# Zero products in the opening of an attention and two-layer kernel: another source, another size, and a later place for the gate sums

## The chip, the cores and the metric

The kernel runs on one core of a Trainium2 chip. The metric is the device time of one execution, in microseconds (us): lower is better. The core has five engines that run their own instruction streams and wait for each other by semaphores: TensorE (PE, matrix products; PEld is its loading of weights), VectorE (DVE), ScalarE (ACT), GpSimd (POOL) and SyncE (SP, which here only issues DMAs).

## What is computed

Four batches of eight heads of causal attention with a decay from gates `f`, then two feed-forward layers over all 2304 tokens, all in float32:

```python
scores = scale * q @ k.T                       # 576 x 576 per head, head_dim 64
cum = cumsum(log(clip(f, 0.0001, 1.0)))        # the gate sums
scores = where(causal, -1e9, scores + cum[:, None] - cum[None, :])
attn = softmax(scores) @ v
x = attn as (2304, 512)
x = leaky_relu(x @ w_in) @ w_out               # 512 -> 2048 -> 512, slope 0.01
out = silu(x @ w2_in) @ w2_out
```

## The kernel before, in words

Python code records the instructions while a small event simulation (class `Plan`) runs: each step says on which engine it runs, a rank and a planned cost, and the simulation decides the order in which steps stand in each engine's stream. The chip then executes these fixed streams. A changed planned cost or a new wait in the recording code therefore changes the order of instructions far beyond the edited line.

When the PE stream would be idle in the simulation, `Plan.issue` records a "filler" instead: a product of zeros into a PSUM tile `fps` that nobody reads. The filler has a planned cost in `p.filler["pe"]`, and once it is over the simulation looks again for real work. On the chip a filler is an ordinary instruction: what stands behind it waits until it is done.

The opening goes like this. `gates` loads the gates (`fs`), takes their logarithm on ACT, and sums them over positions by products with a triangle of constants `tri` (tile `cps`, line 435), in two halves of the sequence: the first 256 positions and the other 320. Both results go through `plain_rows` into `cum_p`, a DRAM row from which later heads load their decay. The first `DIRECT` = 2 heads do not wait for that: `score` adds the decay by further products with `fs` and `tri` (lines 674 and 676, tile `sps`). Other heads compute scores by line 683. DVE takes the maximum out of `sps` (line 663), ACT the exponential (line 706), PE transposes the result (line 765, tile `tps`), and PE multiplies it by the values (line 835, tile `av`). The first eight heads, rows 0 to 255 of batch 0, are done like this before the first product of the first layer (line 965, tile `hps`), which waits for all eight (`wait(("weighed", H - 1))`). The scores of heads 8 and 9, the first two of the next half, are also largely done before it. Meanwhile DVE and ACT convert the weights of the first layer.

Most real products of the opening are float32: each is recorded as two instruction pairs, a load of weights and a product. Products of the first layer use fp32r, one pair each.

Fillers run in two kinds. From the start, `z`, a 128x256 tile that DVE sets to zero, is multiplied by its own first 128 columns (line 398). Once the mask tile `zmask` is complete and the first block of head 0 is scored, 128 zero columns of `zmask` are multiplied with themselves (line 401). They end with the first `hps` product group.

Of the kernel before, what the change touches and what calls it, by code (L numbers as in the profile page):

```python
# [9 lines left out]
F32 = mybir.dt.float32  # L10
F32R = mybir.dt.float32r
# [22 lines left out]
DIRECT = 2  # L34
# [40 lines left out]
class Plan:  # L75
# [39 lines left out]
    def op(self, eng, cost, fn, rank=1, lat=None):  # L115
        def step(resume):
            self.count += 1
            heapq.heappush(self.ready.setdefault(eng, []), (rank, self.count, cost, fn, lat, resume))
            self.at(self.now, lambda: self.issue(eng))

        return step
# [36 lines left out]
    def dma(self, nbytes, fn, rank=1):  # L158
        return self.op("sp", 0.64, fn, rank, nbytes / 360e3)

    def wait(self, *names):
        def step(resume):
            missing = [n for n in names if n not in self.seen]
            if not missing:
                resume()
                return
            left = [len(missing)]

            def one():
                left[0] -= 1  # L170
                if not left[0]:
                    resume()

            for n in missing:
                self.waiting.setdefault(n, []).append(one)

        return step
# [8 lines left out]
    def signal(self, name):  # L186
        self.seen[name] = True
        for fn in self.waiting.pop(name, []):
            fn()

    def take(self, pool, bufs):


        def step(resume):
            i = self.taken[pool] = self.taken.get(pool, -1) + 1
            if i < bufs or (pool, i - bufs) in self.given:
                resume(i)
            else:
                self.queue[pool, i - bufs] = lambda: resume(i)

        return step

    def give(self, pool, i):
        self.given[pool, i] = True
        fn = self.queue.pop((pool, i), None)
        if fn:
            fn()
# [16 lines left out]
def seq(*steps):  # L224
    for step in steps:
        yield step
# [14 lines left out]
def pe_cost(n, passes=1):  # L241
    return passes * n / 2360
# [3 lines left out]
def fused_kernel(ctx, tc, qt, kt, va, vb, ft, w1, wi2, wo2, out):  # L246
    nc = tc.nc
# [12 lines left out]
    p = Plan()  # L260
    op, dma, wait, take, give, signal, par = p.op, p.dma, p.wait, p.take, p.give, p.signal, p.par
# [22 lines left out]
    def f32(ap):  # L284
        return ap.bitcast(F32)
# [8 lines left out]
    def act(n, fn, rank=1, base=0.09):  # L294
        return op("act", act_cost(n, base), fn, rank)

    def dve(n, fn, rank=1, fast=False):
        return op("dve", dve_cost(n, fast), fn, rank)
# [82 lines left out]
    def gates(cp):  # L381
        nfull = S // 128
        rem = S - nfull * 128
        parts = ((128, slice(0, nfull)), (rem, slice(nfull, nfull + 1)))
        fs = cp.tile([128, nfull + 1, H * B], F32, name="fs")
        tri = cp.tile([128, HALF[1][1]], F32, name="tri")
        cp3 = cp.tile([H * B, 2, S], F32, name="cp3")
        cr = cp.tile([H * B, 4, S], F32R, name="cr")
        warm = cp.tile([1, 1], F32, name="warm")
        z = cp.tile([128, 256], F32R, name="z")  # L390
        opened.update(tri=tri, fs=fs, parts=parts, ones=(cp3[:, 0, :], f32(cr[:, 0:2, :])))

        def fillers():
            yield op("dve", 0.28, lambda: nc.vector.memset(f32(z), 0.0), 0)
            i = yield take(("acc", 1), 1)
            fps = ps_acc.tile([128, 256], F32, tag="acc1", name="fps")
            none = zmask[:, 0:128]
            p.filler["pe"] = 0.2, lambda: nc.tensor.matmul(fps, z[:, 0:128], z, start=True, stop=True)
            p.issue("pe")
            yield wait("zmask", ("scored", 0, 0))  # L400
            p.filler["pe"] = 0.21, lambda: nc.tensor.matmul(fps[:, 0:128], none, none, start=True, stop=True)  # L401
            yield wait(("hid", 0, 0))
            del p.filler["pe"]
            give(("acc", 1), i)

        def logs(k):
            n, sl = parts[k]
            if k:
                yield dma(8e3, lambda: nc.sync.dma_start(out=fs[0:n, nfull, :], in_=ft[nfull * 128:S, :]), -1)
            else:  # L410
                yield dma(100e3, lambda: nc.sync.dma_start(
                    out=fs[:, sl, :], in_=ft[0:nfull * 128, :].rearrange("(c p) h -> p c h", p=128)), -3)
            signal(("fs", k))
            yield wait(("clamped", k))
            yield act(128, lambda: nc.scalar.activation(fs[0:n, sl, :], fs[0:n, sl, :], ACTF.Ln), 0)
            signal(("logs", k))

        p.start(fillers())
        p.start(build_consts())
        p.start(logs(0))  # L420
        p.start(logs(1))
        p.start(seq(wait(("logs", 0), ("logs", 1)),
                    op("act", 1.4, lambda: nc.scalar.activation(warm, fs[0:1, 0, 0:1], ACTF.Exp), 0)))
        pss = []
        banks = []
        for i, (t0, tn) in enumerate(HALF):
            yield wait("tri", ("logs", i))
            banks.append((yield take(("av", "sp")[i], (1, 3)[i])))
            ps = ps_at.tile([H * B, tn], F32, tag=("av", "sp")[i], name="cps", bufs=(1, 3)[i])
            todo = [c for c in range(nfull + 1) if t0 <= 128 * c < t0 + tn]  # L430

            def sums(c):
                n = 128 if c < nfull else rem
                lo = 128 * c - t0
                nc.tensor.matmul(  # L435
                    ps[:, lo:tn], fs[0:n, c, :], tri[0:n, 0:tn - lo], start=(c == todo[0]), stop=(c == todo[-1]),
                )

            for piece in ([todo] if i == 0 else [[c] for c in todo]):
                yield op("pe", sum(pe_cost(tn - 128 * c + t0, 4) for c in piece),  # L440
                         lambda: [sums(c) for c in piece], 1 if i else -1)
            pss.append(ps)
            if i == 0:
                p.start(first_rows(ps, first_row["tile"]))
        signal("cum")

        def plain_rows():
            yield wait("rows_set")
            for i, ((t0, tn), ps) in enumerate(zip(HALF, pss)):
                w = slice(t0, t0 + tn)  # L450
                if i == 0:
                    yield act(tn, lambda: nc.scalar.copy(cp3[:, 1, w], ps), 0)
                    yield wait("cf")
                else:
                    yield dve(tn, lambda: nc.vector.tensor_scalar(
                        cp3[:, 1, w], ps, cp3[:, 1, t0 - 1:t0], None, op0=ALU.add), 0)
                give(("av", "sp")[i], banks[i])
            yield dma(147e3, lambda: nc.sync.dma_start(out=cum_p, in_=cp3), 0)
            signal("cum_p")

        def split_rows():
            c, hi, lo = cp3[:, 1], cr[:, 2], cr[:, 3]
            yield act(S, lambda: nc.scalar.copy(hi, c))
            yield dve(S, lambda: nc.vector.tensor_tensor(lo, c, f32(hi), op=ALU.subtract))
            yield dma(295e3, lambda: nc.sync.dma_start(out=cum_d, in_=f32(cr)))
            signal("cum_d")

        yield from plain_rows()
        yield from split_rows()
        yield wait(("scored", DIRECT - 1, 1))  # L470
        signal("gates")

    def first_rows(ps, cf):

        yield wait("ones")
        yield act(256, lambda: nc.scalar.copy(cf[:, 1], ps[0:H]), 0)
        signal("cf")
        yield par(*[seq(
            dma(8e3, partial(nc.sync.dma_start, out=first[i][64:65], in_=cf[2 * i:2 * i + 2]), i - H),
            signals(("row", i)),  # L480
        ) for i in range(DIRECT // 2, H // 2)])
        give("stg", first_row["i"])
        signal("rows")
# [1222 lines left out]
    cp = cum_es.enter_context(tc.tile_pool(name="cump", bufs=1))  # L1706
# [4 lines left out]
    def opening():  # L1711
        first_row["i"] = yield take("stg", STG_BUFS)
        first_row["tile"] = stg([H, 2, HALF[0][1]], F32, "cfr")
        for i in range(5):
            yield take(("w", i), 1)
        p.start(gates(cp), after_gates)
        yield from load_first()
        yield wait(*[("weighed", n) for n in range(H)])
        for i in range(5):
            give(("w", i), 0)  # L1720
# [61 lines left out]
```

## Time and profile before

| | us |
|---|---|
| median of three timed runs | 993.75 |
| the three runs | 993.75, 994.51, 987.34 |
| the profiled execution | 993.82 |
| its span, first to last instruction | 992.1 |
| PE busy | 983.7 |
| DVE busy | 772.6 |
| ACT busy | 648.0 |
| first product of the first layer starts | 44.48 |

Times in the trace count from the start of the span. The busy time of PE is modelled, since products are pipelined. In the chain of waits the piece of a group begins where the piece before it ends, so that its length is what the group added to the chain. [...]

### The profile page before, as it was taken

Reading aid. Unit: us, or ns where it says so; the run is one execution under the profiler, and the core shown is the slowest. Engines: PE = TensorE matmul, PEld = TensorE weight load, DVE = VectorE, ACT = ScalarE, POOL = GpSimd, SP = SyncE. Lnnn points to the kernel's source line nnn. Section 1 sums busy time; section 2 is a strip of 40 time slices with the busy share of each in tenths; the row PEclk is TensorE's granted clock in tenths of the full one; section 3 lists DMA queues with packets and bytes.
Section 4 is the critical chain, followed back from the end, with each engine's and each line's share of the span. In section 5 each row is a group of like instructions: output and inputs, shape, how many; then the busy total and the mean of one; then the engine's idle time right before and its main releaser. Section 6 shows DMA issues by size and latency. Waiting matters only on the chain.

```text
span 992.1 us, 20120 instructions
## 1 busy us (share of the span) xinstructions
PE 983.7 (99%) x7367; PEld 944.9 (95%) x7367; DVE 772.6 (78%) x1837; ACT 648.0 (65%) x1423; POOL 105.5 (11%) x134
## 2 busy tenths in 40 slices
PE   9999999999999999999999999999999999999998
PEld 6877779999999999999999999999999989999998
DVE  3999867878888788887876898557667779899884
ACT  4876767777788767977765567657557765445441
POOL 2000002111222222442211110000000000000000
PEclk9999999999999999999999999999999999999999
DMA  7744523231242221342221675396887984545442
GB/s 228 242 148 123 173 65 108 72 102 41 61 132 78 64 78 46 90 126 64 85 70 57 229 266 202 124 322 214 291 288 271 354 278 122 149 137 161 128 129 64
DMA packets 111831, 148.41 MB, mean 150 GB/s; under 512 B 8170, under 2 KB 89078, under 8 KB 111700
## 3 DMA queue, kind: packets, MB, share of 16 engines
q1 hardware_dynamic: 111300, 146.73, 46.7%
q8 instruction: 58, 0.95, 0.4%
q10 hardware_dynamic: 432, 0.39, 0.1%
q14 instruction: 41, 0.34, 0.1%
HBM read 98.93 MB, written 43.43 MB: 143 GB/s over the span
## 4 chain that ended last, share of the span: by engine, by line
PE 96%; DMA 1%; ACT 1%; DVE 1%; issue 0%; DVEq 0%
PE hps L965 21%; PE acc L1047 19%; PE m L1431 17%; PE m L1277 16%; PE sps L683 7%; PE tps L765 5%; PE av L876 4%; PE acc L1041 3%; PE av L835 2%; PE fps L401 1%; DMA ws<-w_d 1%; DMA g<-g_d 1%; PE sps L676 0%; PE cps L435 0%; PE sps L674 0%
## 5 line engine op out<-in xcount | busy, mean ns | idle before, releaser
L965 PE MATMUL hps<-ring,w 128*128 128x256 f32 x1728 | 261.8, 288 | 0.0
L965 PEld LDWEIGHTS hps<-ring,w 128*128 128x128 f32 x1728 | 229.3, 191 | 4.2 <-issue 2.2
L1047 PE MATMUL acc<-g,dec 128*128 128x256 f32 x1344 | 199.3, 285 | 0.0
L1047 PEld LDWEIGHTS acc<-g,dec 128*128 128x128 f32 x1344 | 177.9, 191 | 0.4
L706 ACT ACTIVATE sc<-sc,st 128x576 f32<-128x576 f32 (+4 forms) x160 | 93.2, 583 | 52.1 <-DVE st L663 50.9
L1277 PE MATMUL m<-xa,w 128*128 128x384 f32 x576 | 113.7, 339 | 0.8 <-DVE ev L1072 0.8
L1431 PE MATMUL m<-w,xa 128*128 128x256 f32 x924 | 112.5, 280 | 0.5 <-DVE xa L314 0.5
L1431 PEld LDWEIGHTS m<-w,xa 128*128 128x128 f32 x924 | 110.4, 188 | 0.7 <-DVE xa L314 0.7
L1277 PEld LDWEIGHTS m<-xa,w 128*128 128x128 f32 x576 | 101.8, 188 | 1.0 <-DVE ev L1072 1.0
L306 ACT CAST dec<-wo 128x512 fp32r<-128x512 f32 x112 | 69.5, 621 | 44.3 <-PE acc L1047 43.5
L663 DVE CUSTOM_DVE_ANT_0 sc<-sps,zmask 128x288 f32<-128x288 f32 (+4 forms) x160 | 72.0, 451 | 30.7 <-PE sps L683 16.4
L1277 PE MATMUL m<-xb,w 128*128 128x384 f32 x432 | 86.6, 337 | 0.8 <-ACT z L1332 0.8
L314 DVE TENSOR_TENSOR dec<-wo,dec 128x512 fp32r<-128x512 f32 x92 | 64.9, 705 | 20.9 <-ACT dec L306 20.4
L306 ACT CAST xa<-g 128x512 fp32r<-128x512 f32 x88 | 49.2, 567 | 46.8 <-PE m L1431 18.5
L1277 PEld LDWEIGHTS m<-xb,w 128*128 128x128 f32 x432 | 76.0, 188 | 1.6 <-ACT z L1332 1.4
L1431 PE MATMUL m<-w,xb 128*128 128x256 f32 x588 | 74.3, 283 | 0.6 <-ACT xb L306 0.4
L1431 PEld LDWEIGHTS m<-w,xb 128*128 128x128 f32 x588 | 72.0, 191 | 1.0 <-ACT xb L306 0.6
L783 DVE TENSOR_TENSOR pl<-tps,pt 107x320 fp32r<-107x320 f32 (+2 forms) x114 | 54.2, 509 | 18.0 <-ACT pt L782 17.1
L1114 DVE TENSOR_TENSOR g<-g 128x256 f32<-128x256 f32 x144 | 59.4, 420 | 10.8 <-DMA g<-g_d 10.1
L765 PE MATMUL tps<-ident,sc 66*107 66x66 f32 (+3 forms) x480 | 66.4, 268 | 0.0
L683 PE MATMUL sps<-m,s 66*128 66x288 f32 (+9 forms) x264 | 59.9, 308 | 0.0
L782 ACT CAST pt<-tps 107x320 fp32r<-107x320 f32 (+2 forms) x114 | 45.9, 446 | 18.6 <-PE tps L765 18.3
(150 smaller groups left out, 1659.2 us busy)
## 6 DMA issues: line engine op xcount, KB each, us to landing
g_d<-z SPq DMA_DIRECT2D x24, 768.0 KB
g<-g_d SPq DMA_DIRECT2D x36, 512.0 KB
w_d<-f SPq DMA_DIRECT2D x16, 896.0 KB
ws<-w_d SPq DMA_DIRECT2D x56, 256.0 KB
wst<-in_wi_dram SPq DMA_DIRECT2D x16, 512.0 KB
wst<-in_wo_dram SPq DMA_DIRECT2D x16, 512.0 KB
qk<-in_kt_dram SPq DMA_DIRECT2D x24, 288.0 KB
wss<-in_w_dram SPq DMA_DIRECT2D x10, 512.0 KB
```

Of the source, the lines that this page charges most:

```text
L306: ("act", act_cost(n, base), lambda: nc.scalar.copy(dst, src), 0.0),
L314: ("dve", dve_cost(n), lambda: nc.vector.tensor_tensor(dst, a, b, op=ALU.subtract), 0.0),
L663: yield dve(w, lambda: nc.vector.tensor_tensor_reduce(out=sc[0:qn, k0:k0 + w], in0=ps[0:qn], in1=zmask[0:qn, z0:z0 + w], scale=-0.125, sca ...
L683: nc.tensor.matmul(ps[0:qn], ht[x][:, qs], ht[y][:, k0:k0 + w], start=r == 0, stop=r == len(ops) - 1)
L706: yield act(kn, lambda: nc.scalar.activation(sc[0:qn, 0:kn], sc[0:qn, 0:kn], ACTF.Exp, scale=-1.0, bias=st[0:qn, 2 * i + a:2 * i + a + 1], ...
L765: nc.tensor.transpose(ps[0:k1 - k0, o:o + qn], ht["p"][i][0:qn, k0:k1], ident[0:qn, 0:qn])
L783: yield op("dve", dve_cost(width), lambda: nc.vector.tensor_tensor(pts[1][0:kw], ps[0:kw], f32(pt[0:kw]), op=ALU.subtract), 0, PE_LAT)
L965: nc.tensor.matmul(hp_t[:, part], w[:, wi, c * 128:(c + 1) * 128], x[xi][:, c, :], start=(part == 0 and c == 0 and r == 0), stop=(c == KC ...
L1047: nc.tensor.matmul(o, w[:, wi, c * 128:(c + 1) * 128], g[:, gi, part * T:(part + 1) * T], start=(start and r == 0 and c % 2 == 0), stop=(s ...
L1114: ("dve", dve_cost(n), lambda: nc.vector.tensor_tensor(dst, a, b, op=op_), 0.0),
L1277: nc.tensor.matmul(dst, w[:, wi, c * 128:(c + 1) * 128], x[:, xi, c], start=start and c == 0 and r == 0, stop=stop and c == 1 and r == 2, ...
L1431: nc.tensor.matmul(banks[b][:, e], t[:, gi, a * 128:(a + 1) * 128], w[:, wi], start=begin and a == 0 and r == 0, stop=jp == NP // 2 - 1 an ...
```

## The change

Four edits. The tile `z` and its setting to zero are gone: the first fillers read a constant of value 0.0 that the program's own start-up writes, as float32, 128 columns by 128, with a planned cost of 0.42 in place of 0.2. The later fillers multiply 64 columns in place of 128, against the same 128 columns of weights, with a planned cost of 0.11 in place of 0.21. The gate sums of the second half are recorded only after the scores of head 1 (`("scored", DIRECT - 1, 1)`). Lines behind these edits are numbered one higher than before, those between them one lower.

```diff
-        z = cp.tile([128, 256], F32R, name="z")
 ...
         def fillers():
-            yield op("dve", 0.28, lambda: nc.vector.memset(f32(z), 0.0), 0)
             i = yield take(("acc", 1), 1)
             fps = ps_acc.tile([128, 256], F32, tag="acc1", name="fps")
             none = zmask[:, 0:128]
-            p.filler["pe"] = 0.2, lambda: nc.tensor.matmul(fps, z[:, 0:128], z, start=True, stop=True)
+            zero = nc.const_aps.tensor(0.0, [128, 128], F32)
+            p.filler["pe"] = 0.42, lambda: nc.tensor.matmul(fps[:, 0:128], zero, zero, start=True, stop=True)
             p.issue("pe")
             yield wait("zmask", ("scored", 0, 0))
-            p.filler["pe"] = 0.21, lambda: nc.tensor.matmul(fps[:, 0:128], none, none, start=True, stop=True)
+            p.filler["pe"] = 0.11, lambda: nc.tensor.matmul(fps[:, 0:64], none, none[:, 0:64], start=True, stop=True)
 ...
             todo = [c for c in range(nfull + 1) if t0 <= 128 * c < t0 + tn]
+            if i:
+                yield wait(("scored", DIRECT - 1, 1))
```

The first place is the start of PE's stream: first fillers, gate sums (`cps`) and the scores of head 0 (`sps`; a row "x15" is fifteen equal instructions in a row, and a float32 product is one row here). Before:

```order
L398 MATMUL fps<-z 128x256 x15
L435 MATMUL cps<-tri,fs 32x256
L435 MATMUL cps<-tri,fs 32x128
L674 MATMUL sps<-qk_116 128x128
L676 MATMUL sps<-tri,fs 128x128
L435 MATMUL cps<-tri,fs 32x320
L674 MATMUL sps<-qk_116 128x256
L676 MATMUL sps<-tri,fs 128x256
L676 MATMUL sps<-tri,fs 128x128
```

After:

```order
L397 MATMUL fps<-const-float32-0.0 128x128 x8
L436 MATMUL cps<-tri,fs 32x256
L436 MATMUL cps<-tri,fs 32x128
L675 MATMUL sps<-qk_115 128x128
L677 MATMUL sps<-tri,fs 128x128
L397 MATMUL fps<-const-float32-0.0 128x128
L675 MATMUL sps<-qk_115 128x256
L677 MATMUL sps<-tri,fs 128x256
L677 MATMUL sps<-tri,fs 128x128
```

Fifteen fillers of 256 columns have become eight of 128, and a ninth stands where the 320 columns of the second gate sum stood.

The second place is PE's stream behind the last score of head 1, up to the second group of transposes (`tps`). Before:

```order
L676 MATMUL sps<-tri,fs 128x128
L401 MATMUL fps<-zmask 128x128 x3
L765 MATMUL tps<-ident,sc 128x128 x3
L401 MATMUL fps<-zmask 128x128
L683 MATMUL sps<-qk_117 128x128
L401 MATMUL fps<-zmask 128x128
L683 MATMUL sps<-qk_117 128x256
L401 MATMUL fps<-zmask 128x128 x3
L765 MATMUL tps<-ident,sc 128x128 x3
```

After:

```order
L677 MATMUL sps<-tri,fs 128x128
L400 MATMUL fps<-zmask 128x64
L436 MATMUL cps<-tri,fs 32x320
L766 MATMUL tps<-ident,sc 128x128 x3
L436 MATMUL cps<-tri,fs 32x192
L684 MATMUL sps<-qk_116 128x128
L436 MATMUL cps<-tri,fs 32x64
L684 MATMUL sps<-qk_116 128x256
L400 MATMUL fps<-zmask 128x64 x3
L766 MATMUL tps<-ident,sc 128x128 x3
```

The three pieces of the second gate sum stand here now, among the first transposes and the scores of head 2, where fillers stood.

The third place is PE's stream behind the values of heads 4 and 5 (`av`), some 10 us before the first layer begins. Before:

```order
L835 MATMUL av<-pf,v_120 64x256 x2
L401 MATMUL fps<-zmask 128x128
L835 MATMUL av<-pf,v_120 64x128 x2
L401 MATMUL fps<-zmask 128x128 x3
L765 MATMUL tps<-ident,sc 128x128 x3
```

After:

```order
L836 MATMUL av<-pf,v_119 64x256 x2
L400 MATMUL fps<-zmask 128x64
L836 MATMUL av<-pf,v_119 64x128 x2
L400 MATMUL fps<-zmask 128x64 x14
L766 MATMUL tps<-ident,sc 128x128 x3
```

Three fillers have become fourteen. Up to the first `hps` row the real PE instructions are the same ones before and after; the fillers of `zmask` number 46 before and 75 after.

## Rows read from the trace of the kernel before

**Rows 1.** The page's first part: busy time of each engine, share of the span, instructions.

```profile
PE 983.7 (99%) x7367; PEld 944.9 (95%) x7367; DVE 772.6 (78%) x1837; ACT 648.0 (65%) x1423; POOL 105.5 (11%) x134
```

**Rows 2.** Waits of PE, whole span: who for whom, total us, times, longest.

```profile
PE fps L398 <- DVE z L394: 1.3, 1, 1.3
PE m L1277 <- ACT z L1332: 0.8, 2, 0.6
...
PE m L1431 <- DVE xb L314: 0.2, 1, 0.2
```

**Rows 3.** Chain of waits, 0 to 24 us: start, length, engine, tile, line, instructions.

```profile
1.26 3.57 PE fps L398 x15
4.83 1.42 PE cps L435 x4
...
7.70 1.21 PE cps L435 x2
...
11.63 0.78 PE cps L435 x2
...
13.86 0.35 PE cps L435 x2
...
16.93 1.28 PE fps L401 x6
18.21 0.64 PE tps L765 x3
18.85 0.43 PE fps L401 x2
...
20.98 0.74 PE fps L401 x6
21.73 0.33 PE tps L765 x3
```

**Rows 4.** Chain of waits, 24 to 47 us.

```profile
26.60 0.67 PE fps L401 x6
...
42.74 1.98 PE fps L401 x16
44.72 0.71 PE hps L965 x6
```

**Rows 5.** Chain of waits, 21.73 to 44.72 us: share of that stretch by line.

```profile
by line: PE fps L401 42.8%; PE sps L683 30.6%; PE av L835 16.6%; PE tps L765 10.0%
```

**Rows 6.** Two stretches: busy us (instructions) of each engine, clock, DMA share, GB/s.

```profile
4.83:16.93 12.10, 12.10 (x31) 6.65 (x32) 1.99 (x10) 4.21 (x12) 3.12 (x8) 1.00 0.86 225
21.73:44.72 22.99, 22.99 (x163) 17.46 (x162) 21.29 (x78) 19.68 (x57) 0.00 (x0) 1.00 0.71 227
```

**Rows 7.** Timeline at 162 us, fp32r products by line 876: start, us, engine, instruction.

```profile
162.25 0.28 PE L876 MATMUL av<-pl,vh 128*128 128x256 f32 x1
...
162.37 0.22 PE L876 MATMUL av<-pt,vh 128*128 128x128 f32 x1
162.37 0.19 PEld L876 LDWEIGHTS av<-pl,vh 128*128 128x128 f32 x1
162.43 0.27 PE L876 MATMUL av<-pl,vh 128*128 128x128 f32 x1
162.48 0.42 PEld L1047 LDWEIGHTS acc<-g,dec 128*128 128x128 f32 x3
162.54 0.45 PE L1047 MATMUL acc<-g,dec 128*128 128x256 f32 x2
```

**Rows 8.** Timeline of the first 1.3 us, instructions of POOL, ACT's queue and DVE.

```profile
0.30 0.10 POOL L1770 MEMSET const-float32-0.0<- 128x1 f32 x1 [0.30 <-issue]
...
0.93 0.27 DVE L394 MEMSET z<- 128x256 f32 x1 [0.93 <-PEq L1770]
```

**Rows 9.** Timeline: issue of `cum_p`, and the first scores that read it.

```profile
16.06 0.39 SPq L458 DMA_DIRECT2D cum_p<-cp  x1
...
36.87 0.70 PE L683 MATMUL sps<-k,s 65*66 65x320 f32 x2
```

## The prediction

> **What bounds the kernel now.** The page's busy times come first: PE is busy 99% of the span, DVE 78%, ACT 65% [rows 1]. PE's waits say how much of its time is lost: 1.3 us at the start, until DVE has set `z` to zero, and then five kinds of waits between 0.8 and 0.2 us each, 2.7 us in all, in the second layer [rows 2]. So PE's stream is the path from 1.26 us on, and whatever is taken out of it or put into it moves the end by as much, unless it opens or fills a wait. The chain of waits of the opening says which parts of that stream are not needed: 3.57 us of `z` fillers, then from 16.93 us on mask fillers between the real products, and 1.98 us of them just before the first layer begins [rows 3, 4]. Between 21.73 and 44.72 us mask fillers hold 42.8% of the chain, 9.84 of 22.99 us, in 38 products [rows 5]. In the same stretch DVE is busy 21.29 us [rows 6]: shorter fillers could win only some 1.7 us there before DVE becomes the bound. Longer fillers have no such limit.
>
> [...]
>
> **The change part by part.** All against the profiled execution, 993.82 us, which is 0.07 above the median of the three runs.
>
> *The constant in place of `z`.* The constant is written at 0.30 us, and engines leave the start-up at about 0.93, where DVE begins [rows 8]. PE starts there instead of at 1.26: -0.33 us. The memset was on DVE, idle then: nothing. Eight float32 fillers of 128 columns at 0.43 [rows 3] are 3.44 us in place of 3.57: -0.13. A ninth one stands in PE's stream before the second score of head 0: +0.43 at the low clock, +0.22 at the high one.
>
> *The gate sums.* The three pieces, 1.21 + 0.78 + 0.35 = 2.34 us [rows 3], move behind the scores of head 1: PE does the same work, so the sum is zero. Behind them wait `cum_p` and, through it, the rows for heads 8 and 9. `cum_p` was issued at 16.06 and first read by a score at 36.87 us [rows 9]; about 5 us of delay fit into the 20.81 us between, and the loads of weights behind `cum_p` on SP's queue keep their order and a similar margin. If that cover were gone, PE would wait at most those 5 us once.
>
> *Mask fillers of 64 columns.* Forty-six become 75, because the planner charges 0.11 us for each and so puts about two where one stood. The question is their price. No row before has 128 columns of weights against 64 moving columns in float32. The upper bound is that of today's filler, 0.22 us (0.67 for three) [rows 4], the lower its half, 0.11. The nearest row decides for the upper one: two fp32r products of 128 columns follow each other at 162.37 and 162.43, the second is recorded 0.05 us longer than the first (0.27 against 0.22), and weight loads follow each other after 0.11 us (162.37, 162.48) [rows 7]. A load of 128 weight columns takes 0.11 us there, and only a product as long as that hides it. A float32 filler has two loads: 0.22 us whatever streams past them. I take 0.22, and 0.43 at the low clock.
>
> [...]
>
> *Where the time goes, if the clock rises at 21 us as before.* Up to the second group of transposes: PE starts at 0.93; 3.44 for the eight; the chain from 4.83 to 21.73 is 16.90 us, of which fillers 1.28 + 0.43 + 0.43 + 0.74 = 2.88, so 14.02 real; the ninth constant filler and six of the mask add 7 x 0.43 = 3.01. Together 0.93 + 3.44 + 14.02 + 3.01 = 21.40, against 21.73: -0.33. From there to the first `hps` product 75 - 6 = 69 fillers stand where 38 stood: 31 x 0.22 = +6.8 us. Sum +6.5: 1000.3 us.
>
> *If it rises early.* The base is the run of 987.34 us. Start and first fillers -0.33 and -0.13, the ninth +0.22, and 29 more mask fillers at 0.22 are +6.4: 993.5 us. That run won 6.4 us, though halving everything from 4.83 to 21 us would win 8.1, so some 1.7 us of PE's time were waits for DVE, ACT and loads; fillers that fall into these cost nothing. That gives 991.8 to 993.5, and I take 992.6.
>
> *Downstream.* The planner's new order also moves conversions between ACT, DVE and POOL in the middle of the kernel. PE has its work ready there in all but 2.7 us [rows 2]; I put it at zero, within 2 us either way.
>
> [...]
>
> **Forecast:** early rise, fillers at the price of their weight loads, 992.6 us, chance 0.50.
>
> **Rival 1, the clock rises at about 21 us.** 1000.3 us, chance 0.24. [...]
>
> **Rival 2, the clock stays low until the first layer: slower.** [...] Then the 22.99 - 9.84 = 13.15 us of real work take 26.3, and 69 fillers 29.7: the first `hps` product starts at 77.4 us and not at 44.72, +32.7. [...] It decides if the rise has not come by the time the mask fillers start. Chance 0.13.
>
> **Rival 3, the half-size filler does cost half.** Late rise: 69 x 0.11 = 7.6 against 9.84 would give -2.2, of which DVE leaves 1.7; six early ones at 0.21 save 1.3; -0.33: 990.5 us. Early rise: 987.34 - 0.33 - 0.13 + 0.22, less 1.9 for 75 x 0.11 against 46 x 0.22, gives 985.2. For it speaks only that the planner's price assumes it; against it the loads at 162 us. Chance 0.13.
>
> **How the numbers follow.** The prediction is the forecast's, 993 us rounded. About 1% is what a measurement of this kernel can tell from no change: 983.8 to 1003.7 us. The forecast, rival 3 and most of rival 1 lie within. Slower is rival 2 with 0.13, and 0.04 of rival 1 where the downstream order adds to it: 0.17. Faster needs rival 3 with an early rise and a gain downstream: 0.05. Same is the rest, 0.78. The range runs from 985, rival 3's lower end, to 1004, rival 1 with a loss downstream; rival 2 alone is outside.
>
> **What would show it.** First `hps` product, in the chain of waits: 42 to 44 us for the forecast, 51 for rival 1, 77 for rival 2, 41 or less for rival 3. A run of fourteen 64-column fillers, 28 instructions: 3.1 us by weight loads, 1.5 by columns, 6 at the low clock. The time of a 128-column transpose group behind the first scores, 0.64 or 0.33 us, shows the clock. PE's first instruction should start near 0.93 us. And PE should still show no wait before the second layer: a wait on DVE or on a DMA before the scores of heads 2 or 8 would mean that fillers are no longer the bound and their price matters less than I say. The forecast is wrong if the first layer starts where I say and the end still differs by more than 2 us: then the downstream order matters.

## Result: slower by 1.2%, and the profile after

The kernel after takes 1000.25 us (median of six runs, 999.45 to 1002.93), before 991.17 (six runs, 986.98 to 994.51): the ratio is 1.0119, 95% interval 1.0091 to 1.0147. Forecast were 993 us and no change. Before's runs lie in two groups, 987 to 989 and about 994 us, after's in one. In the later comparisons before's median is 987.6, and 72 of its 86 runs lie in the lower group; against that after loses 12.7 us.

The profiled execution took 1002.93 us, its span is 1001.2. PE is busy for longer than before [rows 1], with 61 more instruction pairs:

```profile
PE 988.9 (99%) x7428; PEld 950.4 (95%) x7428; DVE 778.5 (78%) x1839; ACT 645.5 (64%) x1418; POOL 106.8 (11%) x136
```

The chain of waits of the opening, to be held against [rows 3] (start, length, engine, tile, line, instructions):

```profile
0.85 3.75 PE fps L397 x16
4.60 1.42 PE cps L436 x4
...
7.08 0.22 PE fps L397 x2
...
11.59 0.66 PE cps L436 x2
12.25 0.48 PE tps L766 x3
...
15.06 0.33 PE tps L766 x3
```

PE starts with the constant at 0.85. The ninth constant filler takes 0.22 us at 7.08, where the eight first took 0.47 each (3.75 / 8). The second gate sum begins with 0.66 us in place of 1.21, the first transposes take 0.48 in place of 0.64, and the second ones 0.33 already at 15.06. In the profile before such transposes take 0.64 us at 18.21 and 0.33 at 21.73, and a mask filler 0.43 at 18.85 and 0.22 at 26.60 us (0.67 for three) [rows 3, 4]; the longer times are called the low clock here, the shorter ones the high clock. So TensorE left the low clock for the high one before 7.08 us, and not at about 21 us as in the profile before. The trace's own record of the granted clock, which lists 1.00 and 0.50 of full speed, begins at 1.00 at 6.4 us after and at 21.0 before, where the times get shorter; ahead of that it lists nothing.

Further on in the same chain, against [rows 4]:

```profile
26.23 2.15 PE fps L400 x18
...
32.74 3.27 PE fps L400 x28
```

Fourteen 64-column fillers, 28 instructions, take 3.27 us, 0.234 each. The timeline shows the first product of the first layer at 44.13 us, 0.35 us earlier than before (start, length, engine, instruction):

```profile
44.13 0.72 PE L966 MATMUL hps<-ring,w 128*128 128x256 f32 x4
```

What the early clock won in the opening the fillers took back. The other 9 us of this execution arose later. PE's waits (who for whom, total us, times, longest), in whose list before has nothing above 0.8 us but its start [rows 2]:

```profile
PE acc L1042 <- DVE wo L1481: 1.9, 1, 1.9
PE acc L1048 <- DVE wr L314: 1.7, 1, 1.7
PE m L1432 <- ACT xb L306: 1.0, 1, 1.0
...
PE m L1432 <- DVE xb L314: 0.7, 2, 0.4
```

Their places in the timeline of PE; the brackets hold the idle time ahead of an instruction and what ended it:

```profile
53.52 0.74 PE L1048 MATMUL acc<-g,wr 128*128 128x256 f32 x2
56.00 0.74 PE L1048 MATMUL acc<-g,wr 128*128 128x256 f32 x4 [1.73 <-DVE wr L314]
...
125.93 1.62 PE L1042 MATMUL acc<-gw,wo 128*128 128x256 f32 x3 [1.85 <-DVE wo L1481]
```

Both are products with the second matrix of the first feed-forward layer, `w_out` ("second-layer weights" in the expectations below), that wait for converted weights: `wr` are the two weight tiles that stay resident, `wo` is the eleventh of the fourteen others that DVE finishes in the first pass:

```profile
125.10 0.68 DVE L1481 SCALAR_TENSOR_TENSOR wo<-wso,ct 128x512 int32<-128x512 int32 x1
```

Here is what the windows show behind the first of them, and over a longer stretch at each (busy us of PE, PEld, DVE, ACT and POOL, then the granted clock):

```profile
56.00:57.50 1.50, 1.50 (x13) 1.50 (x14) 1.49 (x3) 1.50 (x4) 0.00 (x0) 1.00 0.00 0
57.70:61.00 3.30, 3.30 (x15) 2.10 (x14) 3.30 (x8) 2.00 (x4) 0.00 (x0) 0.50 0.00 0
61.20:65.00 3.80, 3.80 (x25) 2.91 (x24) 1.52 (x4) 0.43 (x1) 0.00 (x0) 1.00 0.86 247
...
50.00:70.00 20.00, 18.27 (x100) 12.54 (x99) 17.45 (x45) 11.23 (x25) 0.00 (x0) 0.91 0.44 148
110.00:135.00 25.00, 23.15 (x133) 17.80 (x133) 17.83 (x50) 14.71 (x34) 0.00 (x0) 0.93 0.46 151
```

After the wait, PE had worked for 1.6 us when its granted clock fell to 0.50 of full speed, at 57.6 us in the clock's record, and it came back 3.4 us later. At 0.91 of full speed over 20 us and 0.93 over 25 us, up to 1.8 us are lost at each place, by an estimate from these shares. So the two waits and the two falls make at most 3.6 + 3.5 = 7.1 of the 9.5 us that this execution is longer than before's behind the first layer's start (1002.93 - 44.13 = 958.8 against 993.82 - 44.48 = 949.3). This execution is the longest of after's six, and its mean granted clock, 0.996, the lowest; the others have 0.998 or 0.999.

### The profile page after: what moved, and what is told of

It reads as the page before. It is cut to its first block, busy times and chain, and to the rows that moved or that the text cites. A ratio compares the mean times of both kernels' runs of the same rounds, so it can differ in the third digit from the quotient of the medians.

```text
span 1001.2 us, 20230 instructions
## 1 busy us (share of the span) xinstructions
PE 988.9 (99%) x7428; PEld 950.4 (95%) x7428; DVE 778.5 (78%) x1839; ACT 645.5 (64%) x1418; POOL 106.8 (11%) x136
## 4 chain that ended last, share of the span: by engine, by line
PE 92%; DVE 3%; DMA 2%; ACT 1%; issue 1%; SPq 0%; DVEq 0%; ACTq 0%
PE hps L966 19%; PE acc L1048 18%; PE m L1278 17%; PE m L1432 16%; PE sps L684 6%; PE tps L766 5%; PE av L877 4%; PE acc L1042 2%; PE av L836 2%; PE fps L400 1%; DMA g<-g_d 1%; DMA wss<-in_w_dram 1%; PE fps L397 0%; DVE sc L664 0%; DVE g L1115 0%
## 5 line engine op out<-in xcount | busy, mean ns | idle before, releaser
L306 ACT CAST xa<-g 128x512 fp32r<-128x512 f32 x88 | 49.6, 568 | 46.0 <-PE m L1432 24.2
```

Source lines behind the costliest of these rows:

```text
L306: ("act", act_cost(n, base), lambda: nc.scalar.copy(dst, src), 0.0),
```

## The experiments

Two quantities tell the parts apart in every run: the start of the first `hps` product, and the **rest**, which is the profiled execution's time less that start. The recorded order gives two more. The fillers are those of the mask tile up to the first `hps` product. A maximum is one block of scores reduced by DVE (`sc<-sps,zmask`): counting how many stand ahead of the two `wr` and ahead of the last `wo` in DVE's stream tells how late these conversions are placed. Up to the first `hps` product PE does the same real products in every kernel, but for six transposes more (0.63 to 0.66 us) in e4 and e8.

| kernel | fillers x us each | maxima ahead of wr; last wo | first hps | PE's wait on wr, wo | rest | median |
|---|---|---|---|---|---|---|
| before | 46 x 0.22 | 22, 23; 50 | 44.48 (late clock) | 0, 0 | 949.3 | 987.6 |
| after | 75 x 0.234 | 26, 26; 54 | 44.13 | 1.7, 1.9 | 958.8 | 1000.25 |
| e1 narrow weights | 75 x 0.12 | as after | 41.34 | 1.7, 1.9 | 956.4 | 998.72 |
| e2 same order, 128 columns | 75 x 0.237 | as after | 44.29 | as after | 956.9 | 1001.60 |
| e3 no size | 47 x 0.22 | 22, 22; 50 | 38.23 | 0, 0 | 951.8 | 989.97 |
| e4 size alone | 93 x 0.22 to 0.24 | 24, 26; 56 | 47.58 | 0, 0 | 954.6 | 1001.81 |
| e5 true price | 38 x 0.22 to 0.24 | 22, 24; 54 | 35.64 | 0, 1.8 | 955.5 | 991.53 |
| e8 constant alone | 53 x 0.24 | 22, 24; 50 | 39.88 | 0, 0 | 950.1 | 989.93 |
| e9 planned at 0.13 | 80 x 0.22 to 0.24 | 22, 23; 50 | 45.00 | 0, 0.3 | 949.3 | 994.40 |
| e10 rows first | 83 x 0.22 to 0.24 | 22, 23; 50 | 45.80 | 0, 0.5 | 956.5 | 1002.23 |
| e11 rows late | 45 x 0.22 | 26 and more; 50 | 39.22 | 1.5, 0 | 956.8 | 996.11 |
| e12 before, narrow | 46 x 0.12 | as before | 38.53 | 0, 0 | 950.2 | 988.85 |
| e13 planned at 0.13, narrow | 80 x 0.12 | as e9 | 42.52 | 0, 0.3 | 949.2 | 992.03 |
| e14 no size, narrow | 47 x 0.12 | as e3 | 38.06 | 0, 0 | 952.0 | 990.18 |
| e15 conversions first | 75 x 0.22 to 0.24 | 22, 24; 50 | 43.09 | 0, 0 | 955.7 | 999.45 |
| e16 residents first | 75 x 0.22 to 0.24 | 22, 24; 52 | 43.84 | 0, 0 | 956.9 | 1000.71 |
| e17 before, conversions first | 48 x 0.22 | 21, 24; 50 | 37.32 | 0, 0 | 956.1 | 993.48 |

In all but before's profile the clock rose early, as in after: at 4.1 to 6.8 us by the clock's record. The medians are device times in us; before's is that of the runs shared with the experiments (987.58 to 988.03). The price of a filler is read from its runs in the chain at the high clock; a piece also holds what the first filler of a run waited for, so runs of five and more give 0.21 to 0.26 us with 128 weight columns and 0.12 to 0.14 with 32. The `wo` that PE waits for in after, the eleventh, stands behind 50 maxima in after, e1, e2 and e5, which wait 1.8 to 1.9 us for it, and in e4, which does not; in the other kernels it stands behind 43 to 46.

### First round: which edit, and is it the filler's price?

**e1, narrow weights.** After's order to the instruction, with a cheaper filler:

```diff
-matmul(fps[:, 0:64], none, none[:, 0:64], ...)
+matmul(fps[0:32, 0:64], none[:, 0:32], none[:, 0:64], ...)
```

> The changed kernel with the same order of every engine's instructions; only what a mask filler loads is smaller: 32 weight columns in place of 128 (64 moving columns as before, planned cost 0.11 us as before), so that it writes 32 rows of the unread tile. Theory 'price': the 64-column filler costs 0.23 us on the chip because of its two loads of 128 weight columns, twice what the order was planned with, and the real products, and DVE's and ACT's conversions behind them, run late against the plan. Then a run of 28 filler instructions, 3.3 us in the changed kernel, takes 1.5 to 2 us, the first layer starts 2 to 5 us earlier than at 44.1, the waits of PE near 55 and 125 us go, and the time is 985 to 992 us. Theory 'order': the new order of instructions itself, with the gate sums moved, lets the conversions come too late; then the filler gets cheaper, but the waits near 55 and 125 us stay and the time is 996 to 1000.

Measured: 998.72 us, ratio to before 1.0102 [1.0073, 1.0132]. The chain shows fourteen fillers in 1.68 us, half of after's price:

```profile
31.61 1.68 PE fps L400 x28
```

The first `hps` product came only 2.8 us earlier, and both waits stayed:

```profile
PE acc L1042 <- DVE wo L1481: 1.9, 1, 1.9
PE acc L1048 <- DVE wr L314: 1.7, 1, 1.7
```

So the price is a small part of the loss: 1.5 of 12.7 us.

**e2, after's order with 128 columns.**

```diff
-p.filler["pe"] = 0.11, ... matmul(fps[:, 0:64], none, none[:, 0:64], ...)
+p.filler["pe"] = 0.11, ... matmul(fps[:, 0:128], none, none, ...)
```

> The changed kernel with the same order; only the mask filler streams 128 columns again (128 weight columns, planned cost still 0.11 us). 'Price' by weight loads: the filler costs the same 0.22 to 0.23 us with 64 as with 128 columns, so the time is that of the changed kernel within 2 us (998 to 1003), first layer at 44 us. If instead columns set the price, 75 fillers of 0.11 us more put the first layer at about 50 us or later and the time at 1005 or more.

Measured: 1001.60 us, ratio 1.0133 [1.0104, 1.0162]. The same run of fourteen fillers:

```profile
32.80 3.32 PE fps L400 x28
```

With 64 columns it took 3.27 us. Half of the columns saved 0.05 us in fourteen fillers. (The first `hps` product came 0.16 us later although the clock rose 1.3 us earlier than in after, at 5.1 us; by an estimate from that, half of 1.3 us, the columns were worth some 0.8 us in all 75.)

**e3, the first and the second edit without the third** (128 columns, planned at 0.21).

```diff
-p.filler["pe"] = 0.11, ... matmul(fps[:, 0:64], none, none[:, 0:64], ...)
+p.filler["pe"] = 0.21, ... matmul(fps[:, 0:128], none, none, ...)
```

> The changed kernel without its third edit: mask fillers of 128 columns at a planned 0.21 us, constant and moved gate sums kept; 47 mask fillers up to the first layer. 'Price': plan and chip agree, the clock rises early as in the changed kernel, and the time is that of the quick runs of the kernel before or a little less, 983 to 989 us. 'Order' (the moved gate sums are what costs): 995 to 1001 us.

Measured: 989.97 us, ratio 1.0015 [0.9991, 1.0039]. No wait on `wr` or `wo`.

**e4, the third edit alone**, made in before.

```diff
-p.filler["pe"] = 0.21, ... matmul(fps[:, 0:128], none, none, ...)
+p.filler["pe"] = 0.11, ... matmul(fps[:, 0:64], none, none[:, 0:64], ...)
```

> The kernel before with the third edit alone: mask fillers of 64 columns at a planned 0.11 us, z fillers and gate sums as before; 93 mask fillers up to the first layer. 'Price': 93 at 0.23 in place of 46 at 0.24 us put the first layer some 10 us later where the clock rises at 21 us, 5 us where it rises early, and the waits behind it come: 997 to 1008 us. 'Order' (gate sums moved): the gate sums are not moved here, so no loss, 987 to 994 us.

Measured: 1001.81 us, ratio 1.0133 [1.0104, 1.0162]. The third edit alone loses more than the whole change, and behind the first two it adds 10.3 of the 12.7 us (after against e3). Half as many columns are no loss (with all of them e2 takes 1.35 us longer than after); what is left of this edit is the planned cost of 0.11 and the order that follows from it.

### Second round: the count, or the place of the conversions?

**e5, planned at the measured price.**

```diff
-p.filler["pe"] = 0.11, ... matmul(fps[:, 0:64], none, none[:, 0:64], ...)
+p.filler["pe"] = 0.23, ... matmul(fps[:, 0:64], none, none[:, 0:64], ...)
```

> Changed against the kernel after: the planned cost of the 64-column filler is 0.23 in place of 0.11, which is what it was measured to take (0.234 us). The instruction stays the same; the planner then records 38 of them before the first layer in place of 75, and places the conversions of the two resident second-layer weights (wr) behind 22 and 24 score maxima of DVE in place of 26 and 26. Theory 'planned cost' (the planner's order and count are what costs): the first hps product at 36 to 39 us, no wait of PE on wr, median 985 to 991 us. Theory 'instruction' (64 columns against 128 columns of weights are bad for PE by themselves, whatever their number): waits and falls of the granted clock as after, median 996 to 1002.

Measured: 991.53 us, ratio 1.0032 [1.0018, 1.0047]. Of after's loss 8.7 us are gone with the instruction unchanged. That is half a microsecond above the range of "planned cost". The first `hps` product is the earliest of all runs; the rest is 6.2 us above before's, with one wait on `wo`, which I had not expected:

```profile
PE acc L1042 <- DVE wo L1481: 1.8, 1, 1.8
```

**e9, planned at 0.13**, nothing else.

> Changed against the kernel after: planned cost 0.13 in place of 0.11, nothing else. By accident of the order the planner now records 80 fillers before the first layer, five more than after, but wr stands behind 22 and 23 score maxima. Theory 'late conversions' (about half of the loss is the place of the wr and wo conversions on DVE and ACT, the other half is fillers): fillers cost as after or up to 1.2 us more, the first hps product comes at 44 to 46 us, but PE does not wait on wr, and the time from the first hps product to the end is 949 to 952 us as in the kernel before and without the 64 columns, not 956 as after: median 993 to 998. Theory 'fillers alone' (what comes after the first layer's start is a consequence of the fillers, or of running them at 64 columns): 1000 to 1004, with 956 to 958 us behind the first hps product.

Measured: 994.40 us, ratio 1.0073 [1.0050, 1.0096]. Five fillers more than after, the first `hps` product 0.9 us later, and yet 5.9 us less. The rest is before's to the tenth. PE's list of waits has its start at the top, and `wr` not at all:

```profile
PE fps L397 <- PEq L1771: 0.8, 1, 0.8
PE m L1278 <- DVE ev L1073: 0.8, 1, 0.8
PE m L1432 <- DVE xa L314: 0.5, 1, 0.5
PE acc L1042 <- DVE wo L1481: 0.3, 1, 0.3
```

**e10, the second half's rows first:** the steps that the `wr` conversions wait for in the planner go ahead of others.

```diff
-yield act(S, lambda: nc.scalar.copy(hi, c))
+yield act(S, lambda: nc.scalar.copy(hi, c), 0)
 ...  # likewise rank 0 for the subtraction on DVE and the DMA of cum_d
```

> Changed against the kernel after: the three steps that write cum_d (split_rows: a copy on ACT, a subtraction on DVE, a DMA), for whose end the wr conversions wait in the planner, get rank 0 in place of 1 and so go ahead of first-layer conversions. 64 columns at 0.11 stay; 83 fillers before the first layer in place of 75; wr behind 22 and 23 score maxima. Theory 'late conversions': no wait of PE on wr, 949 to 953 us from the first hps product to the end, median 994 to 999 although there are eight more fillers. Theory 'fillers alone': eight more fillers cost 1.9 us, median 1001 to 1005, and 956 us or more behind the first hps product.

Measured: 1002.23 us, ratio 1.0142 [1.0123, 1.0161]. The `wr` moved and its wait vanished, but the rest stayed at 956.5: against "late conversions". Other waits appeared, on DVE's scaled scores and on a hidden tile:

```profile
PE tps L766 <- DVE sc L715: 1.6, 4, 0.5
...
PE hps L966 <- DVE g L314: 0.7, 1, 0.7
```

**e11, rows late**, in e3: the suspected cause added to a kernel without it.

```diff
+yield wait(("scored", 6, 1))
 c, hi, lo = cp3[:, 1], cr[:, 2], cr[:, 3]
```

> The suspected cause added alone: 128 columns at the planned 0.21 as before, the constant and the later gate sums as after, and the steps that write cum_d wait in the planner for the scores of head 6. 45 fillers before the first layer (47 without that wait), wr behind 26 score maxima and more, as after. Theory 'late conversions': the first hps product at 37 to 39 us, but PE then waits 1 to 2 us on wr and again on wo, 955 to 959 us from the first hps product to the end, median 993 to 997. Theory 'fillers alone': nothing changes against the kernel with the first two edits, 988 to 991, no such wait.

Measured: 996.11 us, ratio 1.0077 [1.0060, 1.0094], 6.1 us above e3. The wait on `wr` came (line numbers are one higher here), the one on `wo` did not, and the rest rose by 5.0 us:

```profile
PE acc L1049 <- DVE wr L314: 1.5, 1, 1.5
```

So a late `wr` goes with a loss; e10 says that an early one is no cure by itself.

### Third round: what is a filler's price worth?

The edit of e1, in three other orders: before (**e12**), e9 (**e13**), e3 (**e14**).

> The kernel before with one edit: its 46 mask fillers load 32 columns of zeros and stream 64 in place of 128 and 128; the planned cost stays 0.21, so that every instruction keeps its place. In the trace of the narrow-weights run such a filler took 0.124 us (nine in 1.12), against 0.22 for the one before. Theory 'DVE takes over': of 46 x 0.1 = 4.6 us only part comes back, since DVE was busy 21.29 of 22.99 us in that stretch; first hps product 1 to 2.5 us earlier than in an execution of before with an early rise of the clock, median 985 to 987. Theory 'fillers bind': the first hps product 4 to 4.6 us earlier, 983 to 984. Theory 'clock': narrow loads keep PE less busy, the clock rises late or falls, and the time is 990 or more.

> Both halves of the loss taken away at once: the order that the planned cost 0.13 gives (80 fillers, no wait on wr or wo; 994.4 us with the 64-column filler) and the filler with 32 weight columns (0.124 us in place of 0.234). Theory 'price and order are two separate parts': the first hps product at 41 to 43 us in place of 45.0, no wait on wr and at most 0.5 us on wo, median 990 to 992. Theory 'narrow loads do nothing once the waits are gone' (DVE binds): 993 to 995.

> The first two edits of the change, the planned cost 0.21, and the filler with 32 weight columns: the order of the kernel without the 64 columns (47 fillers, 989.97 us), at a lower price of each filler. Theory 'DVE takes over': first hps product 36 to 37.5 us in place of 38.2, median 988 to 989.5. Theory 'fillers bind': 47 x 0.1 = 4.7 us come back, first hps product 33.5 us, median 985 to 986. Theory 'clock': 991 or more, with a late rise or a fall.

Measured: 988.85 us [0.9994, 1.0018], 992.03 [1.0026, 1.0054], 990.18 [1.0006, 1.0033]. In e13 the 80 fillers give back 2.5 us at the first `hps` product, as expected there. In e12 and e14 they give nothing, where each theory had expected something ("clock" fails too: it rose at 5.7 us in e12, and both times lie below that theory's). Chain shares by line, 5 us to the first `hps` product, of e3 and then of e14, say why:

```profile
by line: PE fps L400 34.5%; PE sps L684 24.9%; PE av L836 11.5%; PE tps L766 8.4%; PE sps L677 7.6%; PE cps L436 7.6%; PE sps L675 6.3%; PE fps L397 0.7%
```

```profile
by line: PE sps L684 32.4%; PE fps L400 24.7%; PE av L836 11.5%; PE tps L766 10.2%; PE cps L436 7.8%; PE sps L677 7.7%; PE sps L675 6.3%; PE fps L397 0.7%
```

Of 33.2 and 33.1 us, the fillers fell from 11.5 to 8.2, while the scores of line 684 rose from 8.3 to 10.7 and the transposes from 2.8 to 3.4: 3.3 us less there, 3.0 more here. It isn't DVE that takes over, as I had expected, but the real product next to the filler. Pieces of the chain at the same place, of e3 and then of e14, show it:

```profile
14.61 0.33 PE tps L766 x3
14.94 0.22 PE fps L400 x2
15.16 0.22 PE sps L684 x2
```

```profile
14.58 0.48 PE tps L766 x3
15.06 0.23 PE fps L400 x2
15.29 0.42 PE sps L684 x2
```

A single filler with 32 weight columns is no cheaper than one with 128, 0.23 against 0.22 us, and the transposes ahead of it, which stand behind fillers as well, and the score behind it take 0.15 and 0.20 us longer.

**e8, the constant alone.**

```diff
-p.filler["pe"] = 0.2, lambda: nc.tensor.matmul(fps, z[:, 0:128], z, ...)
+p.filler["pe"] = 0.42, lambda: nc.tensor.matmul(fps[:, 0:128], zero, zero, ...)
```

> Only the first edit: the constant in place of z, planned at 0.42; gate sums unmoved, mask fillers of 128 columns at 0.21. The planner's order changes with it: 53 mask fillers before the first layer in place of 46, wr behind 22 and 24 score maxima, so no wait on wr is expected. Theory 'the first edit is free' (as forecast): 986 to 989. Theory 'seven more fillers cost 1.5 us': 988.5 to 990.5, as the kernel with the first two edits (989.97), which would leave nothing for the gate sums.

Measured: 989.93 us, ratio 1.0025 [1.0003, 1.0047], the second theory's size: seven more fillers. With the gate sums moved as well (e3) it is 989.97, so in sum these cost nothing, as forecast; but that is the sum of another order, with a first `hps` product 1.65 us earlier and a rest 1.7 us longer (0.6 us of both are the six transposes).

### Fourth round: the conversions moved, PE's stream kept

**e15** gives all conversions of second-layer weights rank 0 in after, **e16** only the two resident ones, **e17** does as e15 in before.

```diff
-yield from to_f32(t, src, y, t, 1, True)
+yield from to_f32(t, src, y, t, 0, True)
-yield copy(DM, w[:, 0], t)
-yield less(DM, w[:, 1], t, f32(w[:, 0]), "d")
+yield copy(DM, w[:, 0], t, rank=0)
+yield less(DM, w[:, 1], t, f32(w[:, 0]), "d", 0)
 ...  # e16 ends here
-yield from to_f32(wo, src, wo, t, 1, True)
+yield from to_f32(wo, src, wo, t, 0, True)
```

> The kernel after with all conversions of second-layer weights at rank 0 in place of 1. PE's stream stays the same up to eleven rows past the first hps product, with the 75 fillers of 64 columns; on DVE the two wr now stand behind 22 and 24 score maxima in place of 26 and 26, and the last wo of the first pass behind 50 in place of 54. Theory 'late conversions': first hps product at 44 us as in after, no wait of PE on wr or wo, no fall of the granted clock behind them, 949 to 952 us from the first hps product to the end (958.8 in the profiled execution of after): median 993 to 997. Theory 'fillers alone': 999 to 1002. Theory 'anything moved costs': a wait elsewhere takes the place of these two, 997 to 1000.

> As the run with all conversions first, but only the two resident weights (wr) get rank 0; wr behind 22 and 24 score maxima, the last wo behind 52 (54 in after, 50 in before). Theory 'late conversions': the wait on wr is gone with the fall of the clock behind it, 1.7 + 1.7 us; the wait on wo stays in part: median 995 to 998. Theory 'fillers alone': 999 to 1002.

> Control: the kernel before with the same ranks as the run with all conversions first. PE had no wait on wr or wo in before, so earlier conversions have nothing to remove. Theory 'late conversions': no gain, 986.5 to 989.5 (48 fillers in place of 46). Theory 'earlier conversions are a gain of their own': below 985, in which case the gain of the other two runs says nothing about the loss of after.

Measured: 999.45 us [1.0082, 1.0141], 1000.71 [1.0094, 1.0149], 993.48 [1.0024, 1.0062]. "Late conversions" fails: both waits are gone in e15 and e16 (in e16 the one on `wo` too, part of which was expected to stay) and the time is after's. In e15 PE waits at the same place for something else, 1.78 + 0.21 us for attention's scaled exponentials, ahead of which ACT now makes `wr` and `wo` (at 46.5 to 49.6 us), and the clock falls there too (55.3 to 58.7 us in the clock's record):

```profile
54.80 0.45 PE L766 MATMUL tps<-ident,sc 66*107 66x66 f32 x2 [1.78 <-ACT sc L717]
55.47 1.15 PE L766 MATMUL tps<-ident,sc 128*107 128x128 f32 x4 [0.21 <-ACT sc L717]
```

e17 fails its forecast in before, too: its rest rises from 949.3 to 956.1, though PE had no such wait to lose. No run beat before.

## Why the prediction was wrong, step by step

- **Base.** No change was forecast against 993.75 us, the median of three runs of which two lie in the upper group. In all, 75 of before's 92 runs lie in the lower one, and against the early run that the forecast starts from, 987.34, its own 992.6 us are a loss of 5.3.
- **Clock.** Early rise, to which I gave 0.50: right in every profiled execution but before's, at 4.1 to 6.8 us. That the run of 987.34 us rose early, that this won it 6.4 us, and that 1.7 us of waits stood against it, terms of the forecast's sum, no run shows: the one profile of before has the late rise. In its place e12, which has before's order, rose at 5.7 us, with its first `hps` product at 38.53 us and 988.71 us in all.
- **Constant and start.** PE from 0.85 us in place of 0.93; the eight fillers 3.75 us in place of 3.44; the ninth 0.22. Right within 0.3 us.
- **Gate sums.** Free: right in sum (e3 against e8).
- **Price of a 64-column filler.** 0.22 us by its weight loads: right for fillers in a row, 0.234 (e2 shows 0.237 for 128 columns). "Whatever streams past them" is too strong: a single one takes 0.17 us in after (at 15.39 us) and 0.22 in e2 (at 14.99), but in both the next one starts 0.45 us later, so the product between took the difference back. The first `hps` product follows the count: 35.64 us with 38 such fillers, 44.13 with 75, 45.00 with 80, 47.58 with 93, which is 11.94 / 55 = 0.217 us for each. Half of the price before, 0.11 us, which I weighed as the lower bound, is excluded for fillers in a row by the measured 0.234.
- **First `hps` product.** Forecast 42 to 44 us, measured 44.13, at the edge. Against before with an early rise (38.5, by e12, which has before's order) that is 5.6 us: this part of the loss was forecast.
- **Downstream: the step that failed.** "PE has its work ready there in all but 2.7 us; I put it at zero, within 2 us either way." The rest grew by 9.5 us in the profiled execution, and by 7.0 at the medians (1000.25 - 44.13 against 987.6 - 38.5). With the 5.6 us that makes 12.6 of the 12.7 us lost. I read the absence of waits as slack. In every new order but those of e8 and e9 the rest was 2.4 us longer or more.

What the runs show in place of zero: the eleven new orders among them (after, e3, e4, e5, e8 to e11, e15 to e17) have rests of 949.3 to 958.8 us, on average 5.4 above before's, and none lies clearly below it. Kernels of one order agree whatever their filler costs and wherever their first `hps` product lies: before and e12 have 949.3 and 950.2 us, e9 and e13 949.3 and 949.2, e3 and e14 951.8 and 952.0. After, e2 and e1 have 958.8, 956.9 and 956.4, with two falls of the clock, one and none. So in after the order costs some 7 us, of which the two waits are 3.6, and the falls of that execution add about 2. But the place of `wr` and `wo` is not *the* cause, as I came to think after the first round. Where they were moved alone (e10, e15 to e17), others came too late. Only the order of 0.13 (e9, e13) brought the rest back to 949.3 with more fillers than after. So neither the number of fillers nor their price makes the rest; the order does.

What stays open is why e4, e10 and e17 lose 5 to 7 us in the rest, and which property of an order decides. Added up from the traces, PE's idle time behind the first `hps` product is 2.8 us in before and 4.7, 6.1 and 6.4 in these three, in waits of 1.1 us at most over the whole kernel; that is 1.9 to 3.6 us of the loss, and why PE is also busy for longer isn't shown. In e4 only 0.2 us of the idle time lies before 250 us, while its last `wo` was done by 143, so late `wr` and `wo` can't be its reason. That the two groups of before's runs are early and late rises is only my reading; e12's profile speaks for it, with a first `hps` product some 6 us earlier than in before's.

Rival 1 had 1000.3 us, the measured time, but by luck: its clock rises at 21 us, which the profile after excludes. Rivals 2 and 3 are excluded by the clock (high from 6.4 us on in after) and by the filler's price (0.234 us). No run shows the doubled times that rival 2 had up to the first layer: the latest rise, before's, was at 21.0 us. Of my signs, the last one spoke: the first layer starts where I said, and the end differs by more than 2 us.

## What to carry to other kernels

A planned cost in a planner is no measured cost: halving it, with the columns, made fillers in a row no cheaper on the chip (0.234 us with 64 columns, 0.237 with 128), put 29 more of them into the stream and reordered all that follows. The order before had few waits, and none of eleven others was better behind the first layer's start: they lost 0 to 9.5 us, 5.4 on average. They are variants of this one change and not independent, but they say that an edit that reorders needs a price in the sum, not zero. Before costing an instruction by its columns, look for a row that shows its weight load: here fourteen fillers took 3.27 us with 64 columns, 3.32 with 128, and 1.68 with 32 weight columns in place of 128 (after, e2, e1).

## What the runs showed of the hardware that was not expected

- A cheaper filler was worth something only in runs of fillers. Fourteen of them went from 3.27 to 1.68 us with 32 weight columns (after against e1), but single ones between real products took 0.23 in place of 0.22 us, and of the 3.3 us that fillers lost in all, 3.0 came back in the scores and transposes beside them (e3 against e14).
- In after the granted clock fell to 0.50 of full speed for 3.4 us, with PE busy all the time, after a wait of 1.73 us that had ended 1.6 us earlier; at the second place it fell where a wait of 1.85 us ended, at 125.9 us in the clock's record. The order does not decide it. With the same two waits, e2 fell at the first place only and e1 at neither (windows of e2, then of e1), and e1's six executions list mean granted clocks from 0.997 to 1.000:

```profile
50.00:70.00 20.00, 18.27 (x100) 13.09 (x99) 17.48 (x45) 11.08 (x25) 0.00 (x0) 0.91 0.46 154
110.00:135.00 25.00, 23.15 (x143) 17.26 (x142) 18.24 (x52) 15.70 (x37) 0.00 (x0) 1.00 0.49 155
```

```profile
50.00:70.00 20.00, 18.27 (x113) 13.25 (x112) 18.73 (x48) 13.91 (x32) 0.00 (x0) 1.00 0.51 146
110.00:135.00 25.00, 23.15 (x147) 18.46 (x146) 17.71 (x53) 16.79 (x42) 0.00 (x0) 1.00 0.36 112
```
